# One letter of an engine plan: nine key copies moved from VectorE to GpSimd

## Chip, cores and metric

One Trainium2 chip, one of its cores. The time is the device time of one execution in microseconds (us); the table below gives the median of several runs. In the text PE is TensorE, DVE is VectorE, ACT is ScalarE, POOL is GpSimd, and SP is SyncE, which issues nearly all of the DMAs.

## The reference

Attention over 4 batches, 8 heads, 768 positions and 64 channels, followed by a feed-forward layer. Three heads (0, 2, 6) see all earlier positions; the other five see the first 4 positions (the sinks) and the last 64.

```python
causal = rel >= 0                                   # rel = query position - key position
stream_keep = causal & (is_sink | in_win)           # first 4 keys, or the last 64
mask = np.where(retr, full_mask, stream_mask)       # by head
scores = np.where(mask, scale * q @ k.T, -1e9)
a = softmax(scores)
x = (a @ v)                                         # laid out as 3072 tokens x 512
h = x @ w_in                                        # 512 -> 2048
g = h * (1.0 / (1.0 + np.exp(-beta * h)))
out = g @ w_out                                     # 2048 -> 512
```

## The kernel before, in words

The 4 x 768 positions are worked through in eight units of 384 queries, two for each batch; `units[6]`, the seventh, is the first half of the last batch. For every unit the kernel loads q, k and v, casts them to bf16 (tiles `c` and `vb`), turns q and k so that channels lie on partitions (tile `QK`; from the fifth unit on by a transposing DMA, `turn_block`), and multiplies them into scores (tile `sp`). ACT takes the exponential into `es`, DVE multiplies by masks, PE sums and multiplies by v, and DVE scales the result into `xT` (`norm`). The feed-forward layer of the unit follows: PE makes 16 blocks of `h` with four matmuls each (`mm1`, `b<-xT,w_in`), ACT takes a tanh of each (`swish_a`, tile `t`, two buffers), DVE makes `gT` of it (`swish_b`, which reads `t` and the PSUM bank of `h`), and PE multiplies `gT` by `w_out` (`mm2`). An `h` block needs one of four PSUM banks (ring `b`), and it is `swish_b` that frees it.

For heads with sinks, `kp_copy` (line 598) makes a second copy of the keys, `KP`, in which the first 4 columns of each 64-key chunk are the sink keys, and the last columns hold a few edge keys. It is three copies for each of three pairs of heads: in a first half of a batch 128x300, 128x20 and 128x24 elements of bf16, nine instructions in all. The scores of the unit's second burst, op 403 below, are what reads them. `qd_copy` (line 611) makes two further copies of keys and queries into a `k2f` buffer, for the unit's first burst of scores, and `shift_v` moves v down by half a block into `vs`.

The order of the work is written out by hand. The program makes 1112 numbered operations; `SEQUENCE` (line 41) lists them, and each engine runs its own in that order. `CHOICE` (line 97) has a letter for each of the 128 operations that may go to several engines: a for ACT, d for DVE, g for POOL. `_Plan.run` (line 147) walks through `SEQUENCE` with rough costs, gives each operation a planned time, deals buffers and PSUM banks by the earliest planned release (`slot = min(self.free[r])`), and sorts by planned time. Within an engine the planned times only rise, so each engine's own order is that of `SEQUENCE`, whatever the costs are.

The piece of `SEQUENCE` around the change is

```python
    824, 828, 339, 341, 822, 825, 418, 396, 367, 389, 419, 832, 836, 397, 826, 829, 830, 833, 834, 837, 840,
```

- 824, 828, 832, 836, 840: the first five blocks of `h` of the fifth unit (PE); 826 and 830 are the DVE's `gT` of the first two, 825, 829 and 833 the ACT's tanhs, and 822 an eviction of an output block
- 339: a cast of v for the sixth unit, on POOL; 341: `shift_v` of the sixth unit, on DVE (one copy, 64x1536)
- 418: the load of q for the eighth unit, issued by SP; 419: the first of POOL's casts of it
- 396: `kp_copy` for the seventh unit, all nine copies
- 367: SP's two DMAs that turn the sums of the sixth unit into `rec`; DVE's reciprocal of it comes after the fifth `gT`
- 389: the last cast of v for the seventh unit, on POOL
- 397: `qd_copy` for the seventh unit, on DVE

The operation that is chosen for is added at line 1224:

```python
            add(("pool", "dve"), (2.6, 1.15), lambda e: [kp_copy(x, pi, ENG[e]) for pi in kp], port=True,
```

The two numbers are the plan's rough costs on POOL and on DVE. `port=True` makes the plan keep it apart in time from other work on POOL; the chip knows nothing of that. `kp_copy` of the third, fourth and seventh unit is on DVE, that of the fifth, sixth and eighth on POOL.

Of the kernel before, what the change touches and what calls it, by code (L numbers as in the profile page):

```python
# [95 lines left out]
]  # L96
CHOICE = (
    "daagaddadadddadaddaddgggdgdddgaaagaggggdaagdddaddadaagddddgaaddgddaaadagdddaddagggggadggdgdggddgggad"
    "gaadaadaaaadaaaaadaddddaadda"
)  # L100

# [1354 lines left out]
```

## Time and profile before

| | us |
|---|---|
| median of 3 runs (lowest, highest) | 233.35 (232.59, 234.51) |
| the profiled execution, its own time | 233.6 |
| its span, first to last instruction | 231.5 |
| busy in the span: PE / DVE / ACT / POOL | 223.0 / 162.6 / 140.7 / 93.1 |

PE is busy for 96% of the span, DVE for 70%, ACT for 61% and POOL for 40%; the granted clock of PE is 0.999 of its full speed. Times in the views are from the start of the span. A row of a timeline has the start, the length, the engine, the operation with the tile that it writes and those that it reads, how many instructions were merged, and, in brackets, how long the engine had stood idle and what ended that. All instructions have line 121, since a helper records them; so the tiles tell them apart.

### The profile page before, as it was taken

The page shows a single profiled execution, that of the slowest core. Times are in us where ns is not written, and L with a number is a line of the kernel's source. Part 1 is how long each engine was busy: PE and PEld are TensorE (multiplying, and loading weights), DVE is VectorE, ACT ScalarE, POOL GpSimd, SP SyncE. Part 2 cuts the span into 40 slices and gives each one's busy share as a digit, 9 for nine tenths or more (in the row PEclk, how much of TensorE's full clock was granted, in tenths as well). Part 3 has the DMA queues.
Part 4 walks back from the last instruction along what each step waited for, and adds up shares of the span by engine and source line. Part 5 has one row for each costly group of instructions (what it writes and reads, how often), then busy time and mean ns, then how long its engine had stood idle before and what let it go on. Part 6 is the DMA issues. An engine that isn't in the chain of part 4 may idle for free.

```text
span 231.5 us, 6532 instructions
## 1 busy us (share of the span) xinstructions
PE 223.0 (96%) x2589; PEld 127.8 (55%) x2589; DVE 162.6 (70%) x403; ACT 140.7 (61%) x233; POOL 93.1 (40%) x227
## 2 busy tenths in 40 slices
PE   8779999999999999999999979999999999999995
PEld 7555566664544555464654635654655555466543
DVE  4777988888588867965585798885497449177621
ACT  5989978896076378626985158615857447008610
POOL 5517948954957327469256280047300000000000
PEclk9999999999999999999999999999999999999999
DMA  6999999999989979979999963997400105321012
GB/s 203 263 333 366 234 330 348 344 332 238 224 181 266 210 153 232 232 175 231 250 230 206 210 153 133 193 153 156 112 3 0 50 2 163 121 91 45 3 45 91
DMA packets 84264, 42.28 MB, mean 183 GB/s; under 512 B 66042, under 2 KB 77002, under 8 KB 84234
## 3 DMA queue, kind: packets, MB, share of 16 engines
q1 hardware_dynamic: 83962, 41.67, 75.0%
q8 instruction: 20, 0.33, 0.6%
q10 hardware_dynamic: 272, 0.20, 0.3%
q14 instruction: 10, 0.08, 0.1%
HBM read 32.27 MB, written 6.37 MB: 167 GB/s over the span
## 4 chain that ended last, share of the span: by engine, by line
PE 85%; DVE 5%; DMA 5%; ACT 2%; SPq 1%; issue 1%; DVEq 0%; ACTq 0%
PE b L121 74%; PE sp L121 11%; DMA vf<-in_v_dram 3%; DMA q2f<-in_q_dram 2%; DVE xT L121 2%; DVE KP L121 1%; DVE gT L121 1%; ACT es L121 1%; SPq L121 1%; DVE es L121 1%; ACT t L121 0%; DVE k2f L121 0%; DVE vs L121 0%; ACT vb L121 0%; ACT QK L121 0%
## 5 line engine op out<-in xcount | busy, mean ns | idle before, releaser
L121 PE MATMUL b<-xT,w_in 128*128 128x384 bf16 x512 | 90.5, 326 | 1.9 <-DVE gT L121 1.7
L121 DVE SCALAR_TENSOR_TENSOR gT<-t,b 128x384 bf16<-128x384 f32 x128 | 68.7, 550 | 31.2 <-ACT t L121 27.7
L121 ACT ACTIVATE t<-b,beta_h 128x384 f32<-128x384 f32 x128 | 72.9, 584 | 27.0 <-PE b L121 13.4
L121 PE MATMUL b<-w_out,gT 128*128 128x512 bf16 (+2 forms) x400 | 88.9, 371 | 0.0
L121 PEld LDWEIGHTS <-w_in 128*128 128x128 bf16 x512 | 48.6, 98 | 36.0 <-issue 2.4
L121 PEld LDWEIGHTS <-gT 128*128 128x128 bf16 x400 | 37.0, 98 | 40.5 <-issue 1.0
L121 ACT ACTIVATE es<-sp 128x1024 bf16<-128x1024 f32 (+4 forms) x50 | 45.9, 950 | 6.8 <-PE sp L121 6.8
L121 ACT ACTIVATE osb<-b 128x512 f32<-128x512 f32 (+1 forms) x15 | 8.7, 578 | 39.3 <-PE b L121 39.3
L121 POOL CAST c<-wf 128x256 bf16<-128x256 f32 x48 | 19.4, 442 | 15.9 <-DMA wf<-in_k_dram 11.4
L121 PE MATMUL sp<-QK 64*64 64x64 bf16 (+7 forms) x432 | 16.9, 234 | 1.4 <-ACT es L121 0.8
L121 POOL COPY KP<-QK 128x24 bf16<-128x24 bf16 (+5 forms) x32 | 8.0, 292 | 23.1 <-DMA QK<-c 22.8
L121 DVE TENSOR_SCALAR osb<-b 128x512 f32<-128x512 f32 (+1 forms) x10 | 6.7, 675 | 15.0 <-PE b L121 15.0
L121 DVE TENSOR_TENSOR xT<-sp,R 64x384 bf16<-64x384 f32 (+4 forms) x30 | 16.0, 555 | 1.7 <-PE sp L121 1.0
L121 PEld LDWEIGHTS <-QK 64*64 64x64 bf16 (+1 forms) x432 | 11.0, 105 | 10.2 <-issue 8.3
L121 DVE TENSOR_TENSOR es<-es,mask_c 128x128 bf16<-128x128 bf16 (+3 forms) x42 | 12.6, 326 | 4.0 <-ACT es L121 3.9
L121 DVE TENSOR_TENSOR es<-es,mask_s 128x128 bf16<-128x128 bf16 (+8 forms) x34 | 13.6, 426 | 0.7 <-ACT es L121 0.5
L121 PE MATMUL sp<-es,vb 128*64 128x64 bf16 (+5 forms) x245 | 13.3, 234 | 0.0
L121 POOL CAST vb<-wf 128x512 bf16<-128x512 f32 x18 | 10.8, 610 | 5.2 <-DMA wf<-in_v_dram 4.5
L121 PEld LDWEIGHTS <-vb 128*64 128x64 bf16 x257 | 11.4, 111 | 0.7
L121 DVE COPY QK<-b 128x384 bf16<-128x384 bf16 (+1 forms) x13 | 8.6, 676 | 4.2 <-PE b L121 4.1
L121 POOL COPY vs<-vb 64x512 bf16<-64x512 bf16 x19 | 11.2, 622 | 0.3
L121 POOL CAST w_in<-wf 128x512 bf16<-128x512 f32 x16 | 9.9, 653 | 2.7 <-DMA wf<-in_moe_w_in_dram 2.7
(112 smaller groups left out, 203.9 us busy)
## 6 DMA issues: line engine op xcount, KB each, us to landing
out_dram<-osb SPq DMA_DIRECT2D x23, 256.0 KB, 3.9
wf<-in_v_dram SPq DMA_DIRECT2D x18, 256.0 KB, 4.5
wf<-in_moe_w_in_dram SPq DMA_DIRECT2D x4, 1024.0 KB, 8.4
wf<-in_moe_w_out_dram SPq DMA_DIRECT2D x4, 1024.0 KB
R<-rd SPq DMA_DIRECT2D x9, 384.0 KB, 5.6
q2f<-in_q_dram SPq DMA_DIRECT2D x16, 192.0 KB, 4.1
wf<-in_q_dram SPq DMA_DIRECT2D x12, 256.0 KB, 4.0
wf<-in_k_dram SPq DMA_DIRECT2D x12, 256.0 KB, 4.0
```

The lines of the kernel that those rows point to most:

```text
L121: ins = f(*a, **k)
```

## The change

Letter 94 of `CHOICE`, which belongs to operation 396, goes from d to g: the nine copies of `kp_copy` for the seventh unit are issued on POOL, at the place that 396 has among POOL's operations, between 339 and 389. On DVE 397 then follows on 341. `SEQUENCE` stays as it is; the plan counts 2.6 in place of 1.15 for the operation, and its later times move with that.

```diff
 CHOICE = (
-    "daagaddadadddadaddaddgggdgdddgaaagaggggdaagdddaddadaagddddgaaddgddaaadagdddaddagggggadggdgdggddgggad"
+    "daagaddadadddadaddaddgggdgdddgaaagaggggdaagdddaddadaagddddgaaddgddaaadagdddaddagggggadggdgdgggdgggad"
     "gaadaadaaaadaaaaadaddddaadda"
 )
```

## The prediction

> **What bounds the kernel now.** I read first what PE, the busiest engine, waits for, over the span without its first 20 us (the kernel's start, which the change doesn't touch).
>
> ```profile
> engine line waited for: us in total, times, longest us
> PE b L121 <- DVE gT L121: 1.7, 1, 1.7
> ```
>
> The list has one row: after its start, PE has a single wait, and it is for a `gT` of DVE. So whatever isn't this wait can give PE at most crumbs. Second, PE's timeline shows where the wait lies.
>
> ```profile
> 129.57 2.76 PE L121 MATMUL b<-w_out,gT 128*128 128x512 bf16 x12
> 132.18 2.76 PE L121 MATMUL b<-xT,w_in 128*128 128x384 bf16 x16
> 136.65 2.11 PE L121 MATMUL b<-xT,w_in 128*128 128x384 bf16 x12 [1.72 <-DVE gT L121]
> ```
>
> The sixteen matmuls are the first four `h` blocks of the fifth unit; they fill the four PSUM banks, and the fifth block waits until DVE has made the first `gT`. Third, the chain of waits tells what kept DVE.
>
> ```profile
> 131.76 0.63 DVE vs L121
> 132.39 0.03 issue
> 132.42 2.90 DVE KP L121 x9
> 135.33 0.01 issue
> 135.34 0.68 DVE k2f L121 x2
> 136.02 0.03 issue
> 136.05 0.56 DVE gT L121
> 136.61 0.04 issue
> 136.65 2.11 PE b L121 x12
> 138.76 0.57 PE sp L121 x20
> 139.34 5.95 PE b L121 x33
> 145.29 0.78 PE sp L121 x53
> ```
>
> The nine `KP` copies that the change moves are 2.90 us of it, and from 136.65 on the chain is PE again. Nobody needs `KP` yet: its reader is the burst of scores at 145.29. Fourth, the input of that first `gT` had been ready long before, as ACT's timeline shows.
>
> ```profile
> 132.38 0.60 ACT L121 ACTIVATE osb<-b 128x512 f32<-128x512 f32 x1 [5.24 <-PE b L121]
> 133.03 1.23 ACT L121 ACTIVATE t<-b,beta_h 128x384 f32<-128x384 f32 x2
> ```
>
> The two tanhs take 1.23 together, so the first ends near 133.64; its `gT` began at 136.05, 2.4 us later.
>
> **What is removed from DVE.** The copies cost 2.90 us here. Elsewhere the same nine, same shapes, ran in these times, first on DVE (third unit), then on POOL (fifth unit):
>
> ```profile
> 49.08 1.04 DVE L121 COPY KP<-QK 128x300 bf16<-128x300 bf16 x9
> ```
>
> ```profile
> 85.60 2.10 POOL L121 COPY KP<-QK 128x300 bf16<-128x300 bf16 x9 [8.46 <-DMA QK<-c]
> ```
>
> POOL had nothing running at 49.08 (its casts end at 49.01 and begin again at 50.96):
>
> ```profile
> 47.84 1.17 POOL L121 CAST w_out<-wf 128x512 bf16<-128x512 f32 x2
> 50.96 2.29 POOL L121 CAST w_out<-wf 128x512 bf16<-128x512 f32 x4 [1.96 <-DMA wf<-in_moe_w_out_dram]
> ```
>
> At 132.42 it is busy without a break:
>
> ```profile
> 125.58 1.73 POOL L121 CAST vb<-wf 128x512 bf16<-128x512 f32 x3
> 131.58 1.94 POOL L121 CAST c<-wf 128x256 bf16<-128x256 f32 x4 [4.27 <-DMA wf<-in_q_dram]
> 133.47 1.75 POOL L121 COPY vs<-vb 64x512 bf16<-64x512 bf16 x3
> 135.17 0.76 POOL L121 CAST c<-wf 128x256 bf16<-128x256 f32 x2
> 137.05 2.12 POOL L121 CAST c<-wf 128x256 bf16<-128x256 f32 x6 [1.12 <-DMA wf<-in_k_dram]
> ```
>
> So 1.86 of the 2.90 us is DVE standing in POOL's way. What bears on the price is that the whole 2.90 goes from DVE's queue.
>
> **What PE gets of it.** Sixteen matmuls last 2.76 with the last one's 0.326 (its group's mean on the page) modelled to the end, so they are (2.76 - 0.326)/15 = 0.162 apart, and the seventeenth could start at 132.18 + 16 x 0.162 = 134.78. It started at 136.65: 1.87 us lost, and that is all that can be had, although 2.90 leaves DVE.
>
> ```profile
> L121 PE MATMUL b<-xT,w_in 128*128 128x384 bf16 x512 | 90.5, 326 | 1.9 <-DVE gT L121 1.7
> L121 DVE SCALAR_TENSOR_TENSOR gT<-t,b 128x384 bf16<-128x384 f32 x128 | 68.7, 550 | 31.2 <-ACT t L121 27.7
> L121 ACT ACTIVATE t<-b,beta_h 128x384 f32<-128x384 f32 x128 | 72.9, 584 | 27.0 <-PE b L121 13.4
> ```
>
> What is late next? On DVE `vs` ends at 132.39 and the two `k2f` copies, 0.68, at about 133.10; the tanh ends at 133.64; so `gT` runs from 133.67 to 134.22 (0.55), ahead of the 134.78 by 0.56. From there a block costs PE 4 x 0.162 = 0.65, ACT 0.58, DVE 0.55: PE is the slowest of the three, and the ring of four banks doesn't stop it again. That cover of 0.56 is what hides `vs` and `k2f`. They meet POOL's casts as the `KP` copies did; if each of the three copies is held back once by a cast (1.94/4, about 0.49), `gT` starts at 133.10 + 1.47 = 134.57 and ends at 135.12, and PE loses 0.38 of the 1.87. I take no loss, since both are already measured beside busy POOL, and keep 1.49 as the lower end.
>
> Here a rule of the Trainium skill bears (SBUF — State Buffer, "Who interferes with whom"): one port pair is shared by VectorE and GpSimd as a lock, and of a fast VectorE copy and a GpSimd instruction the later one waits for all of the other. The rows 1.04 and 2.90 agree with it, and by it the lower end just given is the one to expect: 232.1 of 233.6.
>
> **What is added to POOL.** The copies need the seventh unit's `QK`. SP issues the last of its three transposes at 125.60, and the one whose landing the profile has took 3.3 us: 128.9.
>
> ```profile
> 125.60 1.30 SPq L121 DMA_TRANSPOSE QK<-c  x1
> ```
>
> ```profile
> DMA to landing us min/median/max: 3.3/3.3/3.3
> ```
>
> By `SEQUENCE` they stand before the third of the three `vb` casts of 125.58. Two casts are done by 126.8; POOL waits until 128.9, copies for 2.10 to 131.0 and makes the third cast (1.73/3 = 0.58) to 131.6. The next work, the q casts, waited for its load until 131.58 anyway. So nine instructions and a wait fit into 4.27 us in which POOL stood idle. The nearest dearer row is the eighth unit's nine copies, which are larger (128x360):
>
> ```profile
> 153.53 2.65 POOL L121 COPY KP<-QK 128x360 bf16<-128x360 bf16 x9 [14.36 <-DMA QK<-c]
> ```
>
> With 2.65 or even DVE's 2.90, POOL is 0.6 to 0.9 late at its q casts, and the 1.12 before 137.05, where it waits for k, takes that up. The cast that now queues behind the wait feeds `vb` of the seventh unit alone. `KP` is ready at 131.0, and 145.29 - 1.87 = 143.42 is when PE wants it. SP's queue gets and loses nothing. The copies' price on POOL is nought; if the cover were gone, 2.1 us of POOL's time would come before the q casts, in the way of nothing that PE reads before 157.84, where it first uses the eighth unit's `QK`:
>
> ```profile
> 157.84 0.61 PE L121 MATMUL sp<-QK 64*128 64x384 bf16 x8
> ```
>
> **The sum.** 233.6 - 1.87 = 231.73 for the profiled execution (span 229.6). Its own time is 0.25 above the median of the runs, so the same gain gives 233.35 - 1.87 = 231.48. I say 231.5, 0.8% less.
>
> **The rivals.** *The gain stops at the reciprocal.* DVE runs a reciprocal of `rec` after the fifth `gT`, and it needs the DMAs of 129.03:
>
> ```profile
> 129.03 1.76 SPq L121 DMA_DIRECT2D rec<-sc  x2
> ```
>
> ```profile
> 139.04 0.34 DVE L121 RECIPROCAL rec<-rec 96x32 f32<-96x32 f32 x1
> ```
>
> It began without a wait; 1.87 earlier, at 137.17, its DMAs have had 6.4 us since their issue ended at 130.79. If they land only at 139, DVE stands still again, and the gain shrinks to nothing: 233.4. Against it: the transposes landed in 3.3. Chance 0.08. *Part of it*: the copies left on DVE are held back by casts, gain 1.0 to 1.5, 232.1. Chance 0.13. *More*: in executions where the collision is worse than in the profiled one, PE's loss is greater too, up to the 2.90: 230.45. Chance 0.05. *Slower*: the plan puts later times on all that follows and deals the PSUM banks anew by planned release. An `h` block dealt a bank that is freed one eviction later than now costs PE a block, 0.65, each time; three of them eat the gain, and seven to nine among the 56 blocks that are left give 234 to 235.5. For it: PE never waits now, so the present deal is a good one. Against it: within an engine the order stays, and banks freed by the same DVE shift together. I put it at 235, chance 0.05. *POOL too slow*: the Trainium skill (GPSIMD Engine Reference, "Engine selection") advises VectorE for elementwise work. The rows' 2.10 against 1.04 bear that out, and yet it would take several us of lateness at 131.58 before PE at 157.84 saw any: 0.01, at no change. That the copies moved aren't those at 132.42 is excluded by the order in `SEQUENCE`.
>
> **How the numbers follow.** The forecast holds 0.68. The bound of 1% (about what a measurement of this kernel can tell from no change) lies at 231.02, only 0.46 under it, while the three runs of before lie from 0.8 below to 1.2 above their median: I give 0.4 of the forecast's cases to the far side. Faster by over 1%: 0.68 x 0.4 + 0.05 = 0.32. Slower: 0.05 and 0.01 for scatter, 0.06. Within 1%: 0.62. The range runs from the case of more, 230.4, to no gain less a little, 233.1; it leaves the slower case out and half of the case without gain.
>
> **What would show it.** Right: PE's list of waits after 20 us is empty or under 0.4; nine `KP` copies on POOL begin near 128.9 and last 2.1; the first `gT` of the fifth unit starts near 133.7; POOL's q casts begin within 0.9 of 131.58; the burst at 145.29 begins near 143.4. Wrong: a wait of PE for `gT` or `t` in a later unit (the banks), DVE idle before the reciprocal, or `k2f` copies much longer than 0.68.

## The result, and the profile after

The changed kernel takes 231.24 us (median of 8 runs, 230.84 to 231.89), the kernel before, measured with it, 232.74 (8 runs, 232.06 to 234.51): a ratio of 0.9926 with a 95% interval of 0.9899 to 0.9953. That is 1.50 us less by the medians; 231.5 had been forecast, a gain of 1.87. Here and below, a ratio leaves out the executions that lie more than 1.5% above the fastest of the same kernel, while the medians count all. The profiled execution has a span of 229.5 us, where the sum said 229.6.

The list of what PE waits for after the first 17 us, in the changed kernel (total in us, times, longest):

```profile
engine line waited for: us in total, times, longest us
PE b L121 <- DVE gT L121: 0.2, 1, 0.2
PE sp L121 <- DVE KP L121: 0.2, 1, 0.2
```

The wait of 1.7 is gone, and no other has come in its place; the two of 0.2 lie ahead of the changed place, at 24 and 68 us. PE's timeline of the same place, in the changed kernel:

```profile
132.07 4.71 PE L121 MATMUL b<-xT,w_in 128*128 128x384 bf16 x28
```

What were 16 matmuls, a gap and 12 more is one row of 28. DVE's timeline and ACT's, in the changed kernel, show how the cover turned out:

```profile
129.03 2.60 DVE L121 TENSOR_TENSOR xT<-sp,R 64x384 bf16<-64x384 f32 x4
131.66 0.56 DVE L121 COPY vs<-vb 64x1536 bf16<-64x1536 bf16 x1
132.25 0.78 DVE L121 COPY k2f<-QK 64x128 bf16<-64x128 bf16 x2
133.54 3.15 DVE L121 SCALAR_TENSOR_TENSOR gT<-t,b 128x384 bf16<-128x384 f32 x5 [0.51 <-ACT t L121]
136.61 0.34 DVE L121 RECIPROCAL rec<-rec 96x32 f32<-96x32 f32 x1
```

```profile
132.92 4.48 ACT L121 ACTIVATE t<-b,beta_h 128x384 f32<-128x384 f32 x7
```

DVE now waits 0.51 for the first tanh, and `gT` starts at 133.54 instead of 136.05; the five `gT` run at the pace of the tanhs. The reciprocal follows without a wait. POOL's timeline:

```profile
125.45 1.17 POOL L121 CAST vb<-wf 128x512 bf16<-128x512 f32 x2
128.90 2.10 POOL L121 COPY KP<-QK 128x300 bf16<-128x300 bf16 x9 [2.27 <-DMA QK<-c]
130.94 0.61 POOL L121 CAST vb<-wf 128x512 bf16<-128x512 f32 x1
132.21 0.74 POOL L121 CAST c<-wf 128x256 bf16<-128x256 f32 x2 [0.66 <-DMA wf<-in_q_dram]
133.25 0.74 POOL L121 CAST c<-wf 128x256 bf16<-128x256 f32 x2 [0.29 <-DMA wf<-in_q_dram]
133.94 1.72 POOL L121 COPY vs<-vb 64x512 bf16<-64x512 bf16 x3
```

The nine copies fill what had been idle time; POOL still waits for the q load after them. Every engine's other instructions are those of before, in the same order.

For what follows, one number is of use that the scatter of the first 130 us doesn't blur: the time from the fifth unit's first `h` block (the row of matmuls `b<-xT,w_in` that begins near 132) to the end of the span, the **stretch** below. It is 231.5 - 132.2 = 99.4 before (to two places 99.36) and 229.5 - 132.07 = 97.4 after (97.42): 1.94 less.

### The profile page after: what moved, and what is told of

Read it like the earlier page. It is cut to its first block, busy times and chain, and to the rows that moved or that the text cites. A ratio compares the mean times of both kernels' runs of the same rounds, so it can differ in the third digit from the quotient of the medians.

```text
span 229.5 us, 6530 instructions
## 1 busy us (share of the span) xinstructions
PE 222.0 (97%) x2589; PEld 126.8 (55%) x2589; DVE 159.3 (69%) x394; ACT 140.8 (61%) x233; POOL 94.2 (41%) x236
## 4 chain that ended last, share of the span: by engine, by line
PE 84%; DMA 4%; ACT 4%; DVE 4%; SPq 1%; issue 1%; ACTq 0%; DVEq 0%
PE b L121 74%; PE sp L121 10%; DMA k2f<-in_k_dram 2%; DMA q2f<-in_q_dram 2%; DVE KP L121 2%; DVE es L121 1%; ACT QK L121 1%; ACT es L121 1%; DVE gT L121 1%; ACT osb L121 1%; SPq L121 1%; ACT c L121 1%; ACT t L121 0%; DVE xT L121 0%; DVE c L121 0%
## 5 line engine op out<-in xcount | busy, mean ns | idle before, releaser
L121 POOL CAST c<-wf 128x256 bf16<-128x256 f32 x48 | 18.6, 425 | 12.8 <-DMA wf<-in_k_dram 11.7
L121 POOL COPY KP<-QK 128x24 bf16<-128x24 bf16 (+5 forms) x41 | 9.8, 282 | 22.5 <-DMA QK<-c 13.5
L121 DVE TENSOR_TENSOR es<-es,mask_c 128x128 bf16<-128x128 bf16 (+3 forms) x42 | 11.9, 308 | 4.2 <-ACT es L121 4.1
L121 POOL CAST w_out<-wf 128x512 bf16<-128x512 f32 x16 | 9.3, 613 | 3.5 <-DMA wf<-in_moe_w_out_dram 3.5
```

The lines of the kernel that those rows point to most:

```text
L121: ins = f(*a, **k)
```

## The experiments

The theory: PE loses what stands in DVE's queue ahead of the first `gT` beyond the slack there, and most of it is the copies' collision with POOL's casts. Its rivals: that the copies' place alone is to blame, collision or not; that VectorE is the wrong engine for them anywhere; and that POOL's queue, once loaded, takes the gain back.

| run | what differs | median (kernel before with it), us | ratio, 95% interval | copies of the unit in question, us | stretch, us |
|---|---|---|---|---|---|
| e1_dve_later | on DVE, after the ninth `gT` | 231.69 (232.82) | 0.9979, 0.9949 to 1.0009 | DVE 1.03 | 97.42 |
| e2_dve_before_norm | on DVE, ahead of `xT` | 234.23 (232.82) | 1.0021, 0.9981 to 1.0062 | DVE 1.04 | 100.22 |
| e3_pool_four_times | on POOL, four times over | 232.82 (232.82) | 1.0006, 0.9971 to 1.0041 | POOL 8.46 | 98.87 |
| e4_one_pair_dve | three of nine on DVE | 231.95, one run (232.95) | | DVE 0.68 | 97.42 |
| e5_two_pairs_dve | six of nine on DVE | 231.96 (232.82) | 0.9966, 0.9933 to 0.9998 | DVE 0.96 | 97.61 |
| e6_eighth_on_dve | the eighth unit's on DVE | 231.84, one run (232.95) | | DVE 1.10 | 97.42 |
| e7_third_on_pool | the third unit's on POOL too | 232.10, one run (232.95) | | POOL 2.18 | 97.41 |
| e8_before_q_late | as before, POOL's q casts later | 232.14 (233.37) | 0.9945, 0.9914 to 0.9977 | DVE 1.04 | 97.42 |
| e9_before_again | the kernel before | 232.87, one run (233.37) | | DVE 1.71 | 98.58 |
| e10_after_again | the changed kernel | 236.79, one run (233.37) | | POOL 2.10 | 97.42 |

The times scatter by more than a microsecond here (the 31 runs of the kernel before beside e1 lie between 231.31 and 235.41), while the stretch repeats to 0.01 wherever PE doesn't wait in it; so the readings rest on the traces, one for each run.

**The same engine, another place** (e1). In `SEQUENCE`, 396 is moved behind 861, the ninth `gT` of the fifth unit; the letter is d, as before.

```diff
-    824, 828, 339, 341, 822, 825, 418, 396, 367, 389, 419, 832, 836, 397, 826, 829, 830, 833, 834, 837, 840,
-    841, 420, 844, 838, 845, 842, 368, 851, 398, 846, 852, 853, 855, 859, 856, 857, 860, 422, 863, 864, 861,
+    824, 828, 339, 341, 822, 825, 418, 367, 389, 419, 832, 836, 397, 826, 829, 830, 833, 834, 837, 840, 841,
+    420, 844, 838, 845, 842, 368, 851, 398, 846, 852, 853, 855, 859, 856, 857, 860, 422, 863, 864, 861, 396,
```

> The nine copies stay on DVE but come after the ninth gT of the fifth unit, so nothing that PE waits for stands behind them at 132. If it was the place in DVE's queue that cost PE 1.87 us: no wait of PE near 134.8, the copies begin near 140 with POOL out of work and last 1.04 in place of 2.90, and the gT behind them come about 1 us late, which costs PE 0 to 0.5: 231.2 to 231.8. If it takes GpSimd to get the gain (VectorE is simply the wrong engine for them): the copies last 2.9 again, PE waits 1 to 2 us a little later, 232.5 to 233.

DVE's timeline of this run:

```profile
138.40 1.20 DVE L121 SCALAR_TENSOR_TENSOR gT<-t,b 128x384 bf16<-128x384 f32 x2 [0.78 <-ACT t L121]
139.52 1.03 DVE L121 COPY KP<-QK 128x300 bf16<-128x300 bf16 x9
```

The copies come to 1.03 and cost PE nothing: the stretch is that of the changed kernel. So GpSimd isn't needed for the gain; it is enough that the copies leave the place ahead of the first `gT`. The times alone don't show it: the medians differ by 1.13, but the ratio's interval reaches 1.0009.

**The same engine, earlier** (e2). 396 stands behind 384 and 383, the last transposes, and ahead of 323, the first `xT` multiplication.

```diff
-    805, 390, 363, 776, 338, 361, 362, 364, 365, 366, 384, 322, 799, 323, 324, 325, 809, 383, 813, 817, 821,
-    824, 828, 339, 341, 822, 825, 418, 396, 367, 389, 419, 832, 836, 397, 826, 829, 830, 833, 834, 837, 840,
+    805, 390, 363, 776, 338, 361, 362, 364, 365, 366, 384, 383, 396, 322, 799, 323, 324, 325, 809, 813, 817,
+    821, 824, 828, 339, 341, 822, 825, 418, 367, 389, 419, 832, 836, 397, 826, 829, 830, 833, 834, 837, 840,
```

> The nine copies stay on DVE but come ahead of the fifth unit's four xT multiplications, near 129.0, in the stretch in which POOL has nothing to do. If 1.86 of the 2.90 us was the collision with POOL's casts: they last 1.04, xT ends about 1.05 later (132.7), PE starts its h blocks 0.6 to 0.7 late and then waits for no gT: 231.9. If the 2.90 is their own price at this place: xT ends at 134.5, PE loses 2.4 there, 233.6.

DVE's timeline of this run:

```profile
133.00 1.04 DVE L121 COPY KP<-QK 128x300 bf16<-128x300 bf16 x9 [3.59 <-DMA QK<-c]
134.07 2.60 DVE L121 TENSOR_TENSOR xT<-sp,R 64x384 bf16<-64x384 f32 x4
```

The copies took 1.04, as the collision theory had it. The expected time was missed all the same: `QK` landed at 133.0 and not at 128.9, DVE stood 3.59 us in its queue waiting for it, and `xT` with all that PE needs came behind. That part of the expectation was wrong because I had taken the landing of the first two traces for a fixed one. The trace is that of the longest of the ten runs, 237.58; the three shortest, 231.74 to 232.18, lie near the 231.9 expected, but there is no trace of them. PE's waits for `xT` in this run:

```profile
PE b L121 <- DVE xT L121: 3.3, 3, 2.5
```

Of the 3.3, 2.5 lie ahead of the stretch and 0.8 in it. The 100.22 is 2.8 over 97.42; most of the 2.0 that are left of it is PE's clock and not the copies' place, as two rows of the table by windows show (the last three columns are the granted clock, the DMA share and GB/s). By an estimate from them the clock cost 2 x 0.45 + 2 x 0.40 = 1.7.

```profile
137.00:139.00 2.00, 2.00 (x9) 0.99 (x7) 1.83 (x4) 1.16 (x2) 1.91 (x4) 0.55 1.32 234
139.00:141.00 2.00, 2.00 (x10) 0.95 (x8) 1.11 (x2) 0.71 (x2) 0.78 (x3) 0.60 0.78 196
```

**The same engine and the same place, without the collision** (e8). SP loads the eighth unit's q (418) after its k (422), and the two DMAs of 367 go ahead of both loads; DVE's and POOL's instructions and their order are those of the kernel before.

```diff
-    824, 828, 339, 341, 822, 825, 418, 396, 367, 389, 419, 832, 836, 397, 826, 829, 830, 833, 834, 837, 840,
-    841, 420, 844, 838, 845, 842, 368, 851, 398, 846, 852, 853, 855, 859, 856, 857, 860, 422, 863, 864, 861,
+    824, 828, 339, 341, 822, 825, 396, 367, 422, 418, 389, 419, 832, 836, 397, 826, 829, 830, 833, 834, 837,
+    840, 841, 420, 844, 838, 845, 842, 368, 851, 398, 846, 852, 853, 855, 859, 856, 857, 860, 863, 864, 861,
```

> The kernel before, all nine copies on DVE and at their old place, but SP loads the eighth unit's q after its k, so that POOL's q casts, which ran beside the copies, begin about 5 us later. If the collision with POOL made PE wait: the copies last 1.04 to 1.4, the first gT of the fifth unit starts 1.5 to 1.9 earlier than before, PE waits 0 to 0.4, and from the fifth unit's first h block to the end it takes 97.4 to 97.9 in place of 99.4; about 231.3. If the copies' place alone does: they last near 2.9 and the 99.4 stays.

DVE's timeline, POOL's and PE's:

```profile
132.34 0.56 DVE L121 COPY vs<-vb 64x1536 bf16<-64x1536 bf16 x1
132.93 1.04 DVE L121 COPY KP<-QK 128x300 bf16<-128x300 bf16 x9
133.99 0.33 DVE L121 COPY k2f<-QK 64x128 bf16<-64x128 bf16 x2
134.35 1.07 DVE L121 SCALAR_TENSOR_TENSOR gT<-t,b 128x384 bf16<-128x384 f32 x2
142.35 1.76 DVE L121 COPY vb<-vb 4x768 bf16<-4x768 bf16 x2 [0.27 <-POOL vs L121]
```

```profile
126.59 1.73 POOL L121 CAST vb<-wf 128x512 bf16<-128x512 f32 x3
138.54 0.74 POOL L121 CAST c<-wf 128x256 bf16<-128x256 f32 x2 [10.22 <-DMA wf<-in_q_dram]
142.27 2.86 POOL L121 CAST c<-wf 128x256 bf16<-128x256 f32 x8
```

```profile
132.75 4.71 PE L121 MATMUL b<-xT,w_in 128*128 128x384 bf16 x28
```

With POOL idle from 128.3 to 138.5 the nine copies take 1.04 and the `k2f` copies 0.33 instead of 0.68, at the old place in DVE's queue, and the stretch is 97.42, the changed kernel's to the last place. This is the run that decides between place and collision: PE waited because DVE's copies met POOL's casts and copies, and each of the two, other place or other time of POOL's work, is a cure. The collision went along with the casts: the two `vb` copies at 142.35, which take 0.67 in the changed kernel, took 1.76 beside them here, where PE waits for nothing behind them. The time falls short of what was expected, 232.14 against about 231.3, with the kernel before at 233.37 beside it.

**A second look at both kernels** (e9, e10), unchanged.

> The kernel before, unchanged, for a second trace. The seventh unit's QK landed at 128.9 in the two first traces and as late as 132.9 in later ones. If that moves the copies against POOL's casts, PE's wait here differs from 1.7 (0.8 to 2.5), and from the fifth unit's first h block to the end it takes 98.2 to 100; if the wait is fixed, 99.4 again.

> The changed kernel, unchanged, for a second trace. Wherever the seventh unit's QK lands between 128.9 and 132.9, PE waits for no gT over 0.2 after 17 us, and from the fifth unit's first h block to the end it takes 97.4.

DVE's timeline of the kernel before in its second trace, and PE's:

```profile
132.37 1.71 DVE L121 COPY KP<-QK 128x300 bf16<-128x300 bf16 x9
134.10 1.10 DVE L121 COPY k2f<-QK 64x128 bf16<-64x128 bf16 x2
135.23 1.02 DVE L121 SCALAR_TENSOR_TENSOR gT<-t,b 128x384 bf16<-128x384 f32 x2
```

```profile
135.84 2.11 PE L121 MATMUL b<-xT,w_in 128*128 128x384 bf16 x12 [0.88 <-DVE gT L121]
```

The same copies cost 1.71 this time, and PE waited 0.88 where it had waited 1.72. The stretch is 98.58. So the loss of the kernel before isn't fixed: against 97.42 it was 1.94 in one trace and 1.16 in the other, and the median's 1.50 lies between. The changed kernel's second trace is longer by what happens before its fifth unit, which begins at 137.66 and so 5.6 us late; the stretch is 97.42 again. The lateness is the granted clock and some waits of PE, those for DVE between 56 and 62 us, as two rows of the table by windows and PE's list of waits in this run show:

```profile
17.00:25.00 8.00, 7.92 (x107) 4.90 (x105) 4.64 (x14) 5.97 (x11) 6.15 (x15) 0.80 1.06 352
60.00:80.00 20.00, 19.30 (x219) 9.53 (x219) 12.57 (x34) 7.87 (x11) 11.32 (x28) 0.91 0.74 164
```

```profile
PE b L121 <- DVE es L121: 1.8, 3, 0.7
PE sp L121 <- ACT es L121: 0.6, 2, 0.4
```

By an estimate from these rows the clock takes 8 x 0.20 + 20 x 0.09 = 3.4 us and the waits 2.4, together 5.8. In the changed kernel's first trace the clock is 1.00 in both windows, and these waits aren't there. That the change lowered the clock isn't likely: e6, with the same instructions up to the eighth unit's copies, had a mean clock of 1.000, and the kernel before had 0.978 in one of the 13 runs beside e10, which took 239.42.

**How much DVE can take** (e4, e5). As the changed kernel, but with the copies of the last pair, or of the last two pairs, on DVE. The line for one pair, and in the second run `pi > 1`:

```diff
-            add(("pool", "dve"), (2.6, 1.15), lambda e: [kp_copy(x, pi, ENG[e]) for pi in kp], port=True,
+            add(("pool", "dve"), (2.6, 1.15), lambda e: [kp_copy(x, pi, dve if n == 6 and pi == 3 else ENG[e]) for pi in kp], port=True,
```

> As the changed kernel, but one of the three pairs of heads (three of the nine copies) is copied on DVE. If DVE has slack before the first gT (0.5 idle in the changed kernel's trace and 0.6 of PE's): the three copies take 0.35 to 1.2, PE's wait is 0 to 0.2, span 229.3 to 229.8. If the loss goes with the share of the copies: a wait of 0.6, span 230.1.

> As the changed kernel, but two of the three pairs of heads (six of the nine copies) are copied on DVE, one pair on POOL. If PE's loss is what is left of DVE's time over its slack before the first gT: the six copies take 0.7 (no collision) to 1.9 (as many collisions as before), PE waits 0 to 1.2, middle 0.6: 231.8. If the loss goes with the share of the copies: 6/9 of 1.87, 1.25: 232.5. If any copy left on DVE restores the whole wait: 233.1.

DVE's timeline with one pair on it, then with two:

```profile
132.67 0.68 DVE L121 COPY KP<-QK 128x300 bf16<-128x300 bf16 x3
133.36 0.32 DVE L121 COPY k2f<-QK 64x128 bf16<-64x128 bf16 x2
133.96 3.15 DVE L121 SCALAR_TENSOR_TENSOR gT<-t,b 128x384 bf16<-128x384 f32 x5 [0.27 <-ACT t L121]
```

```profile
132.19 0.96 DVE L121 COPY KP<-QK 128x300 bf16<-128x300 bf16 x6 [0.15 <-DMA QK<-c]
133.17 0.89 DVE L121 COPY k2f<-QK 64x128 bf16<-64x128 bf16 x2
134.09 1.02 DVE L121 SCALAR_TENSOR_TENSOR gT<-t,b 128x384 bf16<-128x384 f32 x2
```

Three copies leave DVE 0.27 idle before the first `gT`, and PE loses nothing. Six bring the `k2f` copies to their end at 134.06, and PE loses 97.61 - 97.42 = 0.19. With none the idle time was 0.51, with nine the loss 1.16 or 1.94. It is a threshold with a slack ahead of it, and no share of the copies. What counts is the time in DVE's queue and not the number of copies: nine at 1.04 with `k2f` at 0.33 cost nothing in e8, six at 0.96 with `k2f` at 0.89, beside a busy POOL, cost 0.19. (The span of e4, 229.9, is 0.1 over what was expected.)

**How much POOL can take** (e3): the nine copies four times, with the same values.

```diff
-            add(("pool", "dve"), (2.6, 1.15), lambda e: [kp_copy(x, pi, ENG[e]) for pi in kp], port=True,
+            add(("pool", "dve"), (2.6, 1.15), lambda e: [kp_copy(x, pi, ENG[e]) for _ in range(4 if n == 6 else 1) for pi in kp], port=True,
```

> As the changed kernel, with POOL making the nine copies four times over (the same values), 6.3 us more work on POOL ahead of the eighth unit's q casts. If POOL's price is nought because nothing that PE reads early stands behind them: the copies last 8.4 from 128.9, the q casts begin near 137.9, the k casts end near 144, the eighth unit's transposes start at most 0.5 late, PE gains no wait over 0.3, 231.2 to 231.6. If work queued on POOL goes to PE: 233 or more, up to 237.

POOL's timeline, DVE's and PE's:

```profile
132.84 8.46 POOL L121 COPY KP<-QK 128x300 bf16<-128x300 bf16 x36 [3.61 <-DMA QK<-c]
141.24 0.61 POOL L121 CAST vb<-wf 128x512 bf16<-128x512 f32 x1
141.80 1.68 POOL L121 CAST c<-wf 128x256 bf16<-128x256 f32 x4
143.43 1.72 POOL L121 COPY vs<-vb 64x512 bf16<-64x512 bf16 x3
```

```profile
141.65 1.80 DVE L121 COPY vs<-vb 4x1344 bf16<-4x1344 bf16 x1
145.18 0.74 DVE L121 COPY vb<-vb 4x768 bf16<-4x768 bf16 x2 [1.73 <-POOL vs L121]
```

```profile
146.43 0.97 PE L121 MATMUL b<-xT,w_in 128*128 128x384 bf16 x5 [1.40 <-DVE gT L121]
```

My expectation was wrong: PE lost 1.45 of the stretch (98.87), though less than the rival's whole 6.3. Not the q casts were late for anything, but the `vs` copies behind them. DVE's `vb` copies (`sink_v`, line 483) overwrite rows of v that these `vs` copies read, so they must wait for them, 1.73 here; they stand in DVE's queue ahead of the eleventh and later `gT`, and PE waits for those. Much of it is the landing: `QK` came late here too, and counted from the first `h` block (133.07 here, 132.07 in the changed kernel) POOL began 2.9 later than in the changed kernel. By an estimate, the `vs` copies would without this have ended near 142.2 in place of 145.15, about when DVE comes to its `vb` copies (141.30 in the changed kernel, so 142.3 here); by this, the 6.3 us of added work alone would have cost PE next to nothing.

**The same letter in other units** (e6, e7). In the first the eighth unit's copies go to DVE, in the second the third unit's to POOL; both else as the changed kernel.

```diff
-    "daagaddadadddadaddaddgggdgdddgaaagaggggdaagdddaddadaagddddgaaddgddaaadagdddaddagggggadggdgdgggdgggad"
+    "daagaddadadddadaddaddgggdgdddgaaagaggggdaagdddaddadaagddddgaaddgddaaadagdddaddagggggadggdgdgggdggdad"
```

```diff
-    "daagaddadadddadaddaddgggdgdddgaaagaggggdaagdddaddadaagddddgaaddgddaaadagdddaddagggggadggdgdgggdgggad"
+    "daagaddadadddadaddaddgggdgdddgaaagaggggdaagdddaddadaagddddgaaddgddaaagagdddaddagggggadggdgdgggdgggad"
```

> As the changed kernel, with the eighth unit's nine copies on DVE instead of POOL. DVE stands idle 2.3 us before 157.0 and POOL has nothing to do then, so by my theory the copies take 1.1 to 1.5 in that idle time and PE waits for nothing: span 229.3 to 229.8. If nine key copies on DVE cost PE time wherever they are: a wait of 1 to 1.9, span 230.5 to 231.4.

> As the changed kernel, with the third unit's nine copies on POOL as well. PE waits for nothing near 49 us, so by my theory there is nothing to gain, and the w_out casts behind the copies on POOL come up to 2.1 late, against 1.6 idle: PE waits 0 to 0.6, span 229.4 to 230.2. If taking key copies from DVE is worth time wherever they are: span 228.5 or less.

DVE's timeline with the eighth unit's copies on it:

```profile
154.86 1.10 DVE L121 COPY KP<-QK 128x360 bf16<-128x360 bf16 x9
157.49 1.02 DVE L121 SCALAR_TENSOR_TENSOR gT<-t,b 128x384 bf16<-128x384 f32 x2 [1.27 <-ACT t L121]
```

Nine copies on DVE cost PE nothing there: they lie in DVE's idle time and POOL has nothing to do. Nor does taking the third unit's copies from DVE bring anything; near 52 us the scores now wait 0.27 for POOL's `KP`. Both spans (230.0 and 230.4) are a little over the ends of what I had expected; the stretch, at 97.4, shows that this comes from ahead of the fifth unit, where e6 differs in nothing. For e7, whose change lies there, one run doesn't tell a loss of half a microsecond from scatter.

## Why the prediction was right

*PE's one wait is all there is to be had.* Right. 2.90 us left DVE's queue, and the stretch gained 1.94, of which 1.87 is the gap as worked out from the matmuls' spacing. PE's fifth block starts 16 x 0.162 after the first, without a stop.

*The slack ahead of the first `gT`.* Right, with 133.54 against 133.67 foretold. That `vs` and `k2f` might be held back by casts came about in part: `vs` took 0.56 as it does beside an idle POOL, but `k2f` 0.78 in place of 0.32 or 0.33 (e6, e8). It still ended 0.51 ahead of the first tanh, so PE lost nothing, and the lower end, 232.1, didn't come about. As a bound it was too mild: it has each copy held back by one cast, and the last section shows a copy that ran beside six of POOL's casts in a row before it ended. The lock described by the Trainium skill (SBUF — State Buffer, "Who interferes with whom") is borne out in kind. The `xT` multiplications, each with one operand in SBUF, took 2.60 beside POOL's nine copies and 2.60 beside an idle POOL, and the same page has such an instruction outside of the lock. DVE's copies took 1.04 beside an idle POOL and 1.71 or 2.90 beside its casts.

*No price on POOL.* Right for nine copies, whose scores began at 143.24 (143.4 foretold); the reason given was wrong in one point. I named PE's use of the eighth unit's `QK` at 157.84 as the first thing that what queues behind the copies could hold up. It is DVE's `vb` copies, which must wait for the `vs` copies that POOL ends at 133.94 + 1.72 = 135.66:

```profile
141.30 0.67 DVE L121 COPY vb<-vb 4x768 bf16<-4x768 bf16 x2
```

The slack is 5.6 us and not several times that, as the run with the copies four times over showed; 2.1 us fit into it, and into POOL's idle time before it.

*The size.* That 231.5 came so near to 231.24 is in part luck. The kernel before had been taken at 233.35, the median of three runs; over eight it is 232.74, 0.61 less. The gain had been taken at 1.87; the medians differ by 1.50, 0.37 less. The two errors go opposite ways. The profiled execution's 1.87 was taken for every execution's, and the wait of the kernel before was 1.72 in one trace and 0.88 in another, because POOL's work and DVE's copies meet at other moments. But the ratio's interval, 1.1 to 2.4 us, holds 1.87 as well as 1.50, so it isn't shown that the usual gain is smaller than forecast. The ratio's 0.74% lies within 1%, to which 0.62 had been given. *More*, the rival by which other executions collide worse than the profiled one, was right in that the collision varies; the one other trace collided less, and two traces don't tell how far it goes.

*The rivals.* The reciprocal didn't wait (136.61, straight after the fifth `gT`). A new deal of PSUM banks that costs PE blocks isn't there: PE has no wait for a bank after 132. In that rival the sum was off: at 0.65 for each block, 234 to 235.5 is four to six blocks over 231.5, and seven to nine would be 236.0 to 237.3. The Trainium skill's advice to keep elementwise work on VectorE (GPSIMD Engine Reference, "Engine selection") names add, mul and max, and has GpSimd roughly at line rate where there is one input. A copy has one, and its price still favours VectorE, 2.10 against 1.04. The advice says nothing on which queue has the time to spare; here that decided.

## What to carry to other kernels

Look first for what the bounding engine waits for at all; if it is one wait, then its length is about all that a change of what it waits for can gain (1.94 here, for a wait of 1.72), however much work leaves the engine it waits for. Where copies of VectorE and work of GpSimd run beside each other, compare the same instructions elsewhere in the trace with GpSimd idle: if they are shorter there, then shifting either engine's work in time can cure as much as moving it. And when work is put on an idle engine, follow all that queues behind it to the first instruction that must wait for it, on every engine, and count an instruction that overwrites what it reads as well as one that reads what it writes, before calling the price nought.

## What the runs showed of the hardware

The nine DVE copies at one and the same place took 2.90, 1.71 and 1.04 us, by what POOL did meanwhile. POOL's own nine took 2.10 in the changed kernel, 2.12 in e6 and 2.10 in e10, but 2.45 in e7, where DVE's `vs` copy, from 132.56 on, ran beside their end.

One copy can be held back by a whole train of POOL's casts, as far as the times tell. In the kernel before, the fourth unit's nine copies on DVE took 3.56, while POOL made six casts of `c` without a break:

```profile
64.66 3.56 DVE L121 COPY KP<-QK 128x360 bf16<-128x360 bf16 x9 [1.19 <-ACT QK L121]
```

```profile
65.14 2.11 POOL L121 CAST c<-wf 128x256 bf16<-128x256 f32 x6
```

The view of the tile `KP` there has the shortest, the median and the longest of the nine, in ns:

```profile
L121 DVE COPY KP<-QK x9: 159/180/2700, 64.7 to 68.0; 128x360 bf16<-128x360 bf16 x3, 128x24 bf16<-128x24 bf16 x3, 128x36 bf16<-128x36 bf16 x3
```

The first copy took 2.70 and ended at 67.36, just after the last of the casts (67.25). The eighth unit's nine, of the same shapes, took 1.10 in e6 with POOL idle. PE hardly noticed: its longest wait for the fourth unit's copies in the first traces is the 0.2 at 68 us in the changed kernel.

And the seventh unit's transposed `QK` landed at 128.9 in the changed kernel and at 132.9 in e6, whose instructions are the same up to there: SP began to issue the three transposes at 120.23 in one and at 123.03 in the other, and the last of them took 3.3 and 4.3 us to land. A place in a queue that is safe in one trace can thus be 3.59 us of waiting in another (e2); a copy that waits for a DMA is better put behind what others wait for.
